# Loading the first rows on one queue, w1 in column chunks behind them, and the last stores in halves

## The chip, the cores and the metric

The kernel runs on one core of a Trainium2 chip. The metric is the device time of one execution in microseconds (us), lower is better; a number for a kernel is the median of several runs. One execution is also taken by the hardware profiler; its records, grouped in views, are what this document reads.

## The reference

The work is two branches on the same layer-normalised rows, added to the input. With 2048 rows of 640 values and a hidden width of 1536:

```python
xn = _layernorm(x, axis=-1)
a = einsum("bsd,ed->bse", xn, dft_hid_re)          # 640 x 640
b = einsum("bsd,ed->bse", xn, dft_hid_im)
y = einsum("ts,bse->bte", dft_seq_re, a) - einsum("ts,bse->bte", dft_seq_im, b)   # 2048 x 2048
h = gelu(einsum("bsd,df->bsf", xn, w1) + b1)       # 640 x 1536
return x + y + einsum("bsf,fd->bsd", h, w2) + b2   # 1536 x 640
```

Everything is float32.

## The kernel before

TensorE (PE) multiplies in a fast 32-bit format, so each operand is split into a high and a low half: ScalarE (ACT) copies the high half, VectorE (DVE) subtracts it from the value, and a product takes three matmuls, high by high, high by low and low by high (`split`, L160 and L161; `product`, L278 to L280; `hidden`, L304). The order of the work is written out by hand; no scheduler moves it.

**The front.** The first 512 rows are four tiles of 128 rows by 640 (`load_x`, 320 KB each). Before: tiles 0 and 2 are loaded by the queue of SyncE (SP), tiles 1 and 3 by that of ScalarE, each queue issuing its transfers in order. Behind them SyncE issues w1. A column of w1 is 640 inputs by 128 hidden units, held as 128 partitions by 5 chunks of 128, the partitions in four quadrants of 32; `load_w1` loads it with four transfers, one for each quadrant, and for columns 0 and 1 with eight, chunks 0 and 1 ahead of 2 to 4. The raw columns use three buffers in turn. A transfer has one of eight completion semaphores in turn, so SyncE issues one only when the transfer eight places earlier on that semaphore has landed.

While the rows come, PE runs ten warm-up matmuls on zeros (`NWARM`, L676). Then, for each tile: its mean (`ln_stats` on VectorE for tiles 0 and 2, `sum_on_act` on ScalarE for 1 and 3), the rows less the mean (`center`, L705, or L716 on ScalarE), five transposes on PE (`transpose_x`, L693) into five PSUM banks. The first column of w1 is split in two parts, chunks 0 and 1 and then 2 to 4 (L728, L729), on ScalarE and VectorE, both ahead of the splits of the five transposed banks (L160, L161). After that PE runs the units: `hidden(0)`, `hidden(1)`, `hidden(2)` of 15 matmuls each, on columns 0, 1, 2 of w1. `hidden(0)` follows the order `FIRST`, which asks for the halves as they become ready. Column 1 is split by `prep_w1(1)`, column 2 by the lines L752 and L758; behind L752 ScalarE copies the first unit's sum (L753) and spreads the row scales over a tile (L755), which PE transposes (L764, `spread`) inside `hidden(2)`, after `ASIDE` = 1 of its matmuls. From there on come the GELU of unit 0 and the first second-layer matmuls, then one unit after another with a hidden and a second-layer part. SyncE's order behind w1's columns 0 to 2 is w2's first tile, the bias b1, two more tiles of w2, then columns 3 and 4.

**The tail.** The Fourier branch works on blocks of 512 output rows; the last pair of blocks comes out as column pairs in the sums `u1`, `u2` and a fifth column. For the last block `in_two` transposes a pair in 32x32 squares on VectorE (L1332), adds it (L452) and stores it with four transfers, one for each quadrant (`store`, L1309). Before: the first pair is stored by SyncE, the second by ScalarE's queue, the fifth column by GpSimd (POOL). Last of all come two single columns of the block before (L1329, L1750), the second of which waits for PE's last matmul; each is stored by SyncE and ScalarE, two transfers each. `end` adds a saved column to a PSUM bank ahead of PE's last fifteen matmuls.

Of the kernel before, what the change touches and what calls it, by code (L numbers as in the profile page):

```python
# [10 lines left out]
F32 = mybir.dt.float32  # L11
# [5 lines left out]
Q = 4  # L17
B = 32
EPS = 1e-5
NWARM = 10  # L20
TAIL = 4
ASIDE = 1
PADL = 8


# [1 line left out]
def kernel(  # L27
# [126 lines left out]
    def split(hi, lo, src, perm=False):  # L154

        h, l, s = (hi, lo, src)
        if perm:
            h, l = chunked(hi), chunked(lo)
            s = src.rearrange("p (q c i) -> p q c i", q=Q, i=B)
        nc.scalar.activation(h, s, AF.Copy)  # L160
        nc.vector.tensor_tensor(l, s, h.bitcast(F32), op=ALU.subtract)  # L161
# [8 lines left out]
    def rows_of(ap, t):  # L170
        return ap[t * TB : (t + 1) * TB].rearrange("(n r) d -> r n d", r=B)
# [4 lines left out]
    def load_x(c, eng=nc.sync):  # L176
        xt[c] = row_tile(f"x{c}")
        eng.dma_start(xt[c], x[c * P : (c + 1) * P])  # L178
# [66 lines left out]

    W1, W2, w1r, w2r = {}, {}, {}, {}

    def load_w1(i, eng=nc.sync, cuts=(0, ND)):
        if i >= NF:
            return  # L250
        t = early.tile([P, ND, P], F32, tag="w1r", bufs=3, name=f"w1r{i}")
        w1r[i] = t
        v = w1.rearrange("(q c i) f -> q i c f", q=Q, i=B)
        for c0, c1 in zip(cuts, cuts[1:]):
            for q in range(Q):
                eng.dma_start(t[q * B : (q + 1) * B, c0:c1], v[q, :, c0:c1, i * P : (i + 1) * P])  # L256

    def load_w2(i, eng=nc.sync):
        if i >= NF:
            return  # L260
        t = early.tile([P, D], F32, tag="w2r", bufs=3, name=f"w2r{i}")
        w2r[i] = t
        eng.dma_start(t, w2[i * P : (i + 1) * P, :])
# [43 lines left out]
        return acc  # L307


    FIRST = [(0, 0), (0, 2), (1, 0), (1, 2), (0, 1), (2, 0), (2, 2), (1, 1), (3, 0), (3, 2)]  # L310
    FIRST += [(2, 1), (4, 0), (4, 2), (3, 1), (4, 1)]

    def gelu(g, acc, fill=lambda k: None):
# [338 lines left out]

    zeros = rows.tile([P, TB], F32, tag="yt", bufs=2, name="zeros")

    RB = rows.tile([P, TB], F32, tag="yt", bufs=2, name="rb")

    for c in range(NC):
        load_x(c, nc.scalar if c % 2 else nc.sync)
    for tag, size, keys in PLACES:
        t = whole[tag] = place(tag, (P, size // 4))  # L660
        for k, key in enumerate(keys):
# [1 line left out]
    nc.gpsimd.memset(eps, EPS)  # L663
    make_identity(nc, ident)
    nc.vector.memset(zeros, 0.0)
    warm = whole["as"][:, :TB]
    nc.vector.tensor_copy(warm, zeros)

    nc.scalar.activation(eps[:, 1:2], eps[:, 0:1], AF.Sqrt)
    load_w1(0, cuts=(0, 2, ND))  # L670
    load_w1(1, cuts=(0, 2, ND))

    wacc = bank(0)

    def warm_up():
        nc.tensor.matmul(wacc, warm[:, :P], warm, start=True, stop=True)  # L676

    for k in range(NWARM):
        warm_up()
    load_w1(2)  # L680
    load_w2(0)
    nc.sync.dma_start(b1c, b1.rearrange("(i p) -> p i", p=P))
    load_w2(1)
    load_w2(2)
    for j in range(ND):
        new_xt(0, j)
    tacc = [bank(3 + j) for j in range(ND)]
# [35 lines left out]
    sum_on_act(3)  # L723
    center(3, ALU.add, MV[:, 3, 5:6], 0, 2)
    center(3, ALU.add, MV[:, 3, 5:6], 2, ND)
    for lo, hi in ((0, 2 * P), (2 * P, D)):
        h, l = (W1[0][:, k, lo:hi] for k in range(2))
        nc.scalar.activation(h, first_w1[:, lo:hi], AF.Copy)  # L728
        nc.vector.tensor_tensor(l, first_w1[:, lo:hi], h.bitcast(F32), op=ALU.subtract)  # L729
    transpose_x(0, 0, ND)  # L730
    transpose_x(1, 0, ND)
    warm_up()
    for j0, j1 in ((0, 2), (2, ND)):
        transpose_x(2, j0, j1)
        transpose_x(3, j0, j1)
    for j in range(ND):
        split(XT[j][:, 0], XT[j][:, 1], tacc[j])
    load_w1(3)
    load_w1(4)
    for q in range(Q):  # L740
# [562 lines left out]
            for k in names:  # L1303
                nc.sync.dma_start(part_of(t, k), sums[t, k])

    def store(t, src, c0, c1, on_act=0, queues=None):

        for q in range(Q):
            (queues[q] if queues else nc.scalar if q >= Q - on_act else nc.sync).dma_start(  # L1309
                rows_of(out, t)[:, :, q * DQ + c0 : q * DQ + c1], src[q * B : (q + 1) * B]  # L1310
            )

    def reload(lo, w, which="xab"):
# [225 lines left out]
    def hidden_beside(b, n):  # L1539


        ta, tb = blocks[b - 1][1], blocks[b][1]
        last = b == len(blocks) - 1
        x_, y_, z_ = (banks[:, k : k + 2] for k in (X, Y, Z))
        us, vs = bank(US), bank(VS)
        ya = yo[ta]

        def s(which, k):
            return sums[(ta, tb)[which], k]

        def t2(k):
            return lambda: add(s(1, KU[k]), s(1, KV[k]), s(1, KU[k]), ALU.subtract)

        def t3(k):
            return lambda: add(s(0, KU[k]), s(1, KU[k]), s(0, KU[k]), ALU.subtract)

        def t4(k):
            return lambda: add(s(0, KV[k]), s(0, KV[k]), s(1, KU[k]), ALU.subtract)

        def columns(k):  # L1560

            return s(1 if last else 0, ("u1", "u2")[k]).rearrange("p a b -> p (a b)").rearrange("p (n e) -> p n e", n=NB)

        def load_yb(k):
            return lambda: nc.sync.dma_start(columns(k), ys[k][tb])

        def copy(dst, src):
            return lambda: nc.scalar.activation(dst, src, AF.Copy)

        def to(dst, acc, name, then=lambda: None):  # L1570


            def f():
                add_turned(dst, turned(acc, name))
                then()

            return f

        def out_a(c0, c1):
            return lambda: store(ta, ya[:, :, c0:c1], c0, c1) if last else None  # L1580

        def odd():
            yt = turned(us, f"yo_{tb}")
            add_turned(ya[:, :, 4 * B :], yt)
            add_turned(yo[tb, 4], yt)
            out_a(4 * B, DQ)()

        def in_two(k):

            acc, name = s(1, ("v2", "v1")[k]), f"yb{k}_{tb}"  # L1590

            def f():
                if name not in A:
                    A[name] = turned(acc, name)
                else:
                    add_turned(columns(k), A.pop(name))
                    out_b(k)()

            return f

        def out_b(k):
            return lambda: store(tb, columns(k), 2 * k * B, 2 * (k + 1) * B, Q if last and k == 1 else 0)

        def last_columns():

            A["end"] = A["rt2"][:, 0, 0, 0]
            nc.vector.transpose(A["end"].rearrange("p (n i) -> p n i", i=B), ya[:, :, 3 * B : 4 * B])

        yb1, yb2 = in_two(0), in_two(1)
        yb4 = to(  # L1610
            yo[tb, 4], vs, f"yb4_{tb}", lambda: store(tb, yo[tb, 4], 4 * B, DQ, queues=[nc.gpsimd] * Q if last else None)
        )
        f5s = [lambda u=u: f5(u) for u in range(2)] if not last else [lambda: None] * 2
        f6s = [lambda u=u: f6(u) for u in range(2)] if not last else [lambda: None] * 2
        v1 = lambda: add(s(1, "v1"), s(1, "v1"), x_)
        end = lambda: add(bank(X + 1), bank(X + 1), A["end"])
        pre = [v1] if n == 17 and not last else []
        post = {

            0: [lambda: gather(1, tb, "v1", z_), lambda: gather(1, tb, "v", vs, op=ALU.subtract), f5s[0]],  # L1620
            1: [f5s[1]],
            3: [to(ya[:, :, : 2 * B], x_, f"ya1_{ta}")],
            2: [last_columns] if last else [],
            4: [t2(0)],
            5: [t2(1)],
            6: [to(ya[:, :, : 2 * B], y_, f"ya2_{ta}", out_a(0, 2 * B)), t2(2)],
            7: [odd],
            8: [t3(0)],
            9: [copy(s(1, "v1"), z_), t3(1)],
            10: [t3(2)],  # L1630
            11: [t4(0)],
            12: [copy(s(1, "v2"), x_), t4(1)],
            13: [load_yb(0), t4(2), load_yb(1)] if last else [t4(2)],
            14: [lambda: add(s(1, "v2"), s(1, "v2"), z_), yb1],
            15: [yb1] if last else [load_yb(0)],
            16: [] if last else [load_yb(1)],
            17: [v1, end, yb2, yb2] if last else [yb1, yb2],
            18: [yb4] if last else [yb2],
            19: [f6s[0]],
            20: [] if last else [f6s[1], yb4],  # L1640
        }.get(n, [])
        if not last:
            if n in (12, 13):
                post.insert(0, lambda: load_g(b, (NW - 1) * ND + 13 - n))
            if n == 18:
                post[:0] = [lambda k=k: load_part(blocks[b + 1][1], k) for k in ("u1", "u")]
            if n == 20:
                post.append(lambda: load_a(put_off[0]))

                def end():  # L1650
                    to(ya[:, :, 2 * B : 4 * B], x_, f"ya3_{ta}")()
                    store(ta, ya, 0, DQ)

                later.append(end)
        return pre, post
# [129 lines left out]
```

## Time and profile before

| | before |
|---|---|
| median of 3 runs | 852.13 us (851.18 to 852.75) |
| profiled execution, own time | 852.08 us |
| its span in the profile | 850.3 us |
| granted TensorE clock | 0.999 |

The profile's page gives busy time of each engine, the chain of work that ended last and the costliest groups; other views answer for a stretch of time, a tile or an engine's waits. PEld is PE's weight load, which overlaps its matmuls; SPq and ACTq are the issue of transfers on SyncE's and ScalarE's queues. DMA share is the mean busy share of the 16 DMA engines that all queues use.

### The profile page before, as it was taken

Reading aid. Unit: us, or ns where it says so; the run is one execution under the profiler, and the core shown is the slowest. Engines: PE = TensorE matmul, PEld = TensorE weight load, DVE = VectorE, ACT = ScalarE, POOL = GpSimd, SP = SyncE. Lnnn points to the kernel's source line nnn. Section 1 sums busy time; section 2 is a strip of 40 time slices with the busy share of each in tenths; the row PEclk is TensorE's granted clock in tenths of the full one; section 3 lists DMA queues with packets and bytes.
Section 4 is the critical chain, followed back from the end, with each engine's and each line's share of the span. In section 5 each row is a group of like instructions: output and inputs, shape, how many; then the busy total and the mean of one; then the engine's idle time right before and its main releaser. Section 6 shows DMA issues by size and latency. Waiting matters only on the chain.

```text
span 850.3 us, 10328 instructions
## 1 busy us (share of the span) xinstructions
PE 841.5 (99%) x3707; PEld 694.6 (82%) x3707; DVE 666.5 (78%) x837; ACT 355.5 (42%) x499; POOL 48.4 (6%) x70
## 2 busy tenths in 40 slices
PE   8999999999999999999999999999999999999997
PEld 6888888878888888888888888888888888888885
DVE  6675766776758888779988887889967998885686
ACT  7554634456665544343444343232323433322241
POOL 0000311031211400000000000000000000000001
PEclk9999999999999999999999999999999999999999
DMA  6667699837679999858644679563855789704464
GB/s 180 187 184 193 156 224 253 197 87 186 205 247 348 353 193 173 174 129 188 154 137 110 162 234 289 145 150 98 208 163 171 253 193 229 300 19 180 126 181 96
DMA packets 207363, 158.45 MB, mean 186 GB/s; under 512 B 80976, under 2 KB 180816, under 8 KB 206800
## 3 DMA queue, kind: packets, MB, share of 16 engines
q1 hardware_dynamic: 198720, 135.38, 62.3%
q0 software_dynamic: 4080, 20.97, 6.2%
q10 hardware_dynamic: 4512, 1.44, 0.7%
q8 instruction: 29, 0.48, 0.3%
q14 instruction: 22, 0.18, 0.1%
HBM read 114.76 MB, written 42.99 MB: 186 GB/s over the span
## 4 chain that ended last, share of the span: by engine, by line
PE 98%; DMA 1%; ACT 0%; DVE 0%; SPq 0%; issue 0%; ACTq 0%
PE banks L278 29%; PE banks L279 29%; PE banks L280 29%; PE banks L304 10%; DMA x<-in_A_x_dram 1%; DMA w1r<-in_B_w_dram 0%; PE banks L336 0%; PE banks L339 0%; PE banks L337 0%; DVE yo L1750 0%; ACT xab L728 0%; ACT xtt L160 0%; PE banks L764 0%; SPq L178 0%; SPq L256 0%
## 5 line engine op out<-in xcount | busy, mean ns | idle before, releaser
L278 PE MATMUL banks<-as,xab 128*128 128x512 f32 x411 | 159.9, 389 | 0.0
L279 PE MATMUL banks<-as,xab 128*128 128x512 f32 x411 | 159.9, 389 | 0.0
L280 PE MATMUL banks<-as,xab 128*128 128x512 f32 x411 | 159.9, 389 | 0.0
L160 ACT ACTIVATE as<-r 128x1024 fp32r<-128x1024 f32 x80 | 85.0, 1062 | 177.4 <-PE banks L280 152.7
L161 DVE TENSOR_TENSOR as<-r,as 128x1024 fp32r<-128x1024 f32 x80 | 97.2, 1215 | 41.6 <-ACT as L160 41.5
L279 PEld LDWEIGHTS banks<-as,xab 128*128 128x128 f32 x411 | 77.2, 188 | 16.0
L278 PEld LDWEIGHTS banks<-as,xab 128*128 128x128 f32 x411 | 77.2, 188 | 16.0
L280 PEld LDWEIGHTS banks<-as,xab 128*128 128x128 f32 x411 | 77.2, 188 | 16.0
L278 PE MATMUL banks<-as,xc 128*128 128x512 f32 x224 | 87.1, 389 | 0.0
L279 PE MATMUL banks<-as,xc 128*128 128x512 f32 x224 | 87.1, 389 | 0.0
L280 PE MATMUL banks<-as,xc 128*128 128x512 f32 x224 | 87.1, 389 | 0.0
L160 ACT ACTIVATE as<-rt 128x1024 fp32r<-128x1024 f32 x32 | 34.0, 1063 | 70.5 <-PE banks L280 62.5
L304 PE MATMUL banks<-xtt,xab 128*128 128x512 f32 x240 | 57.2, 391 | 0.3 <-ACT xtt L160 0.3
L304 PEld LDWEIGHTS banks<-xtt,xab 128*128 128x128 f32 x240 | 44.7, 188 | 10.2 <-ACT xtt L160 0.7
L279 PEld LDWEIGHTS banks<-as,xc 128*128 128x128 f32 x224 | 42.1, 188 | 8.8
L280 PEld LDWEIGHTS banks<-as,xc 128*128 128x128 f32 x224 | 42.1, 188 | 8.7
L278 PEld LDWEIGHTS banks<-as,xc 128*128 128x128 f32 x224 | 42.1, 188 | 8.7
L161 DVE TENSOR_TENSOR as<-rt,as 128x1024 fp32r<-128x1024 f32 x32 | 38.8, 1211 | 5.3 <-ACT as L160 5.3
L160 ACT ACTIVATE as<-u 128x1024 fp32r<-128x1024 f32 (+1 forms) x24 | 22.1, 919 | 48.2 <-PE banks L280 48.2
L512 DVE STREAM_TRANSPOSE r<-raw 128x1024 f32<-128x1024 f32 x32 | 39.5, 1239 | 2.5 <-PE banks L280 1.9
L161 DVE TENSOR_TENSOR as<-u,as 128x1024 fp32r<-128x1024 f32 (+1 forms) x24 | 24.9, 1041 | 18.8 <-ACT as L160 18.8
L512 DVE STREAM_TRANSPOSE rt<-raw 128x1024 f32<-128x1024 f32 x32 | 38.8, 1230 | 0.9 <-PE banks L280 0.8
(351 smaller groups left out, 1615.9 us busy)
## 6 DMA issues: line engine op xcount, KB each, us to landing
raw<-in_A_dft_seq_re_dram SPq DMA_DIRECT2D x64, 256.0 KB, 5.6
raw<-in_A_dft_seq_im_dram SPq DMA_DIRECT2D x64, 256.0 KB, 5.1
ws<-wit SPq DMA_DIRECT2D x15, 384.0 KB, 4.6
xs<-x SPq DMA_DIRECT2D x64, 80.0 KB, 1.8
xo<-in_A_x_dram SPq DMA_DIRECT2D x16, 320.0 KB, 6.4
xab<-wit SPq DMA_DIRECT2D x13, 384.0 KB, 4.7
wit<-wstp POOLq DMA_DIRECT2D x12, 384.0 KB, 3.7
x<-in_A_x_dram SPq DMA_DIRECT2D x14, 320.0 KB, 4.5
```

Source lines behind the costliest of these rows:

```text
L160: nc.scalar.activation(h, s, AF.Copy)
L161: nc.vector.tensor_tensor(l, s, h.bitcast(F32), op=ALU.subtract)
L278: nc.tensor.matmul(acc, wh, mh, start=first, stop=False, skip_group_check=goes_on)
L279: nc.tensor.matmul(acc, wh, ml, start=False, stop=False, skip_group_check=goes_on)
L280: nc.tensor.matmul(acc, wl, mh, start=False, stop=last, skip_group_check=goes_on)
L304: nc.tensor.matmul(acc, W1[i][:, a, j * P : (j + 1) * P], XT[j][:, b], start=n == 0, stop=n == len(steps) - 1)
L512: nc.vector.transpose(held(pieces[g][2], u).rearrange("p c (n i) -> p c n i", i=B), r.rearrange("p n (c i) -> p c n i", i=B))
```

## The change

All four row tiles are issued by SyncE. For columns 0 to 7 `load_w1` issues five transfers, one for each chunk over all 128 partitions; the others keep four by quadrant, so that the number of transfers in all is the same. The zeros of the warm-up matmuls are held three times, in the three raw buffers of w1: the first six matmuls read the first, two more the second, and one after the transposes of tiles 0 and 1 the third. A column's first transfer so waits for the matmuls that read its buffer. The loads of column 2, of w2 and of the bias follow that last warm-up in the program. The second part of the first column's split moves behind the splits of two transposed banks. `FIRST` asks for the low half of bank 1 earlier, and the spread comes after two matmuls instead of one.

At the end the first pair is stored by GpSimd. The second pair is transposed, added and stored in two halves of eight row groups: the first half by SyncE and ScalarE, the second by GpSimd, with `end` between them. The fifth column's four transfers go to SyncE, ScalarE and GpSimd (two).

```diff
-NWARM = 10
+NWARM = 8
+NGATE = (6, 8)
-ASIDE = 1
+ASIDE = 2
...
-    def load_w1(i, eng=nc.sync, cuts=(0, ND)):
+    def load_w1(i, eng=nc.sync):
...
         v = w1.rearrange("(q c i) f -> q i c f", q=Q, i=B)
-        for c0, c1 in zip(cuts, cuts[1:]):
-            for q in range(Q):
-                eng.dma_start(t[q * B : (q + 1) * B, c0:c1], v[q, :, c0:c1, i * P : (i + 1) * P])
+        if i < 8:
+            for c in range(ND):
+                eng.dma_start(t[:, c], v[:, :, c, i * P : (i + 1) * P])
+            return
+        for q in range(Q):
+            eng.dma_start(t[q * B : (q + 1) * B], v[q, :, :, i * P : (i + 1) * P])
...
-    FIRST = [(0, 0), (0, 2), (1, 0), (1, 2), (0, 1), (2, 0), (2, 2), (1, 1), (3, 0), (3, 2)]
+    FIRST = [(0, 0), (0, 2), (1, 0), (1, 2), (0, 1), (1, 1), (2, 0), (2, 2), (3, 0), (3, 2)]
...
+    warms = [early.tile([P, TB], F32R, tag="w1r", bufs=3, name=f"warm{k}") for k in range(3)]
...
     for c in range(NC):
-        load_x(c, nc.scalar if c % 2 else nc.sync)
+        load_x(c)
...
-    warm = whole["as"][:, :TB]
-    nc.vector.tensor_copy(warm, zeros)
+    for warm in warms:
+        nc.vector.tensor_copy(warm, zeros)
...
-    load_w1(0, cuts=(0, 2, ND))
-    load_w1(1, cuts=(0, 2, ND))
+    load_w1(0)
+    load_w1(1)
...
-    def warm_up():
+    def warm_up(k):
+        warm = warms[sum(k >= n for n in NGATE)]
         nc.tensor.matmul(wacc, warm[:, :P], warm, start=True, stop=True)
     for k in range(NWARM):
-        warm_up()
-    load_w1(2)
-    load_w2(0)
-    nc.sync.dma_start(b1c, b1.rearrange("(i p) -> p i", p=P))
-    load_w2(1)
-    load_w2(2)
+        warm_up(k)
...
-    for lo, hi in ((0, 2 * P), (2 * P, D)):
-        h, l = (W1[0][:, k, lo:hi] for k in range(2))
-        ...
+    split_first(0, 2)
     transpose_x(0, 0, ND)
     transpose_x(1, 0, ND)
-    warm_up()
+    warm_up(NWARM)
+    load_w1(2)
+    load_w2(0)
+    nc.sync.dma_start(b1c, b1.rearrange("(i p) -> p i", p=P))
+    load_w2(1)
+    load_w2(2)
...
     for j in range(ND):
         split(XT[j][:, 0], XT[j][:, 1], tacc[j])
+        if j == 1:
+            split_first(2, ND)
...
         def out_b(k):
-            return lambda: store(tb, columns(k), 2 * k * B, 2 * (k + 1) * B, Q if last and k == 1 else 0)
+            return lambda: store(tb, columns(k), 2 * k * B, 2 * (k + 1) * B, [nc.gpsimd] * Q if last else None)
+
+        def last_two():
+            acc, yt = s(1, "v1"), A["yt"](f"yb2_{tb}")
+            d = columns(1).rearrange("p n (e i) -> p e n i", i=B)
+            v1()
+            for n in range(2):
+                m = slice(n * TB // 2, (n + 1) * TB // 2)
+                for e in range(2):
+                    nc.vector.transpose(yt[:, e, m], acc[:, e, m])
+                dn = d[:, :, n * NB // 2 : (n + 1) * NB // 2]
+                add(dn, dn, yt[:, :, m].rearrange("p e (n i) -> p e n i", i=B))
+                queues = [nc.gpsimd] * Q if n else [nc.sync, nc.scalar] * 2
+                store(tb, columns(1), 2 * B, 4 * B, queues, n * NB // 2, (n + 1) * NB // 2)
+                if n == 0:
+                    end()
...
-            yo[tb, 4], vs, f"yb4_{tb}", lambda: store(tb, yo[tb, 4], 4 * B, DQ, queues=[nc.gpsimd] * Q if last else None)
+            yo[tb, 4], vs, f"yb4_{tb}", lambda: store(tb, yo[tb, 4], 4 * B, DQ, queues=[nc.sync, nc.scalar, nc.gpsimd, nc.gpsimd] if last else None)
...
-            17: [v1, end, yb2, yb2] if last else [yb1, yb2],
+            17: [last_two] if last else [yb1, yb2],
```

More of the change, by code (lines that the diff above doesn't have):

```diff
@@ L725, with split_first @@
     center(3, ALU.add, MV[:, 3, 5:6], 2, ND)
-    for lo, hi in ((0, 2 * P), (2 * P, D)):
-        h, l = (W1[0][:, k, lo:hi] for k in range(2))
-        nc.scalar.activation(h, first_w1[:, lo:hi], AF.Copy)
-        nc.vector.tensor_tensor(l, first_w1[:, lo:hi], h.bitcast(F32), op=ALU.subtract)
+    def split_first(lo, hi):
+        h, l = (W1[0][:, k, lo * P : hi * P] for k in range(2))
+        nc.scalar.activation(h, first_w1[:, lo * P : hi * P], AF.Copy)
+        nc.vector.tensor_tensor(l, first_w1[:, lo * P : hi * P], h.bitcast(F32), op=ALU.subtract)
+    split_first(0, 2)
     transpose_x(0, 0, ND)
     transpose_x(1, 0, ND)
-    warm_up()
+    warm_up(NWARM)
[4 more added lines that the diff above has]
+    load_w2(2)
     for j0, j1 in ((0, 2), (2, ND)):
@@ L1304, in put, with store @@
                 nc.sync.dma_start(part_of(t, k), sums[t, k])
-    def store(t, src, c0, c1, on_act=0, queues=None):
+    def store(t, src, c0, c1, queues=None, n0=0, n1=NB):
         for q in range(Q):
-            (queues[q] if queues else nc.scalar if q >= Q - on_act else nc.sync).dma_start(
-                rows_of(out, t)[:, :, q * DQ + c0 : q * DQ + c1], src[q * B : (q + 1) * B]
+            (queues[q] if queues else nc.sync).dma_start(
+                rows_of(out, t)[:, n0:n1, q * DQ + c0 : q * DQ + c1], src[q * B : (q + 1) * B, n0:n1]
             )
```

## The prediction

> **What bounds the kernel now.** I read the page first: span, busy shares, the chain that ended last.
>
> ```profile
> span 850.3 us, 10328 instructions
> PE 841.5 (99%) x3707; PEld 694.6 (82%) x3707; DVE 666.5 (78%) x837; ACT 355.5 (42%) x499; POOL 48.4 (6%) x70
> PE 98%; DMA 1%; ACT 0%; DVE 0%; SPq 0%; issue 0%; ACTq 0%
> ```
>
> TensorE (PE) carries the span. The waits view of PE for the whole run has only three rows (who waited, for whom, us in total, times, longest); the windows view behind it (stretch, us, then busy time of PE, PEld, DVE, ACT, POOL, granted clock, DMA share, GB/s) shows the two ends:
>
> ```profile
> PE banks L676 <- DVE as L667: 1.9, 1, 1.9
> PE banks L693 <- DVE xp L705: 0.5, 1, 0.5
> PE banks L304 <- ACT xtt L160: 0.3, 1, 0.3
> ```
>
> ```profile
> 0.00:10.00 10.00, 7.41 (x31) 5.43 (x31) 5.39 (x14) 5.18 (x10) 0.94 (x8) 1.00 0.53 174
> ...
> 844.00:850.30 6.30, 0.28 (x2) 0.00 (x0) 0.72 (x1) 0.00 (x0) 0.62 (x1) 0.92 0.68 114
> ```
>
> All three waits lie ahead of the first real matmul; from there PE never waits until its last one at about 844.3. So the time is three pieces: the front up to the dense run, the dense run, the tail of 6.0 us. The change leaves the dense matmuls as they are, so only front and tail can move it, and whatever delays PE in the first units goes straight into the total. The chain of waits for the first 12 us (start, us, what) says what ends last in the front:
>
> ```profile
> 1.19 5.58 DMA x<-in_A_x_dram
> ...
> 7.14 1.93 DMA w1r<-in_B_w_dram
> ...
> 9.18 0.53 ACT xab L728
> 9.70 0.49 ACT xtt L160
> ...
> 10.24 1.90 PE banks L304 x7
> ```
>
> The third row tile lands at 6.77. A w1 transfer on SyncE waited for that, was issued at 7.14 and landed 1.93 us later; the second part of w1's first split (L728) waited for it, and the first split of the transposed rows (L160) stands behind that on ScalarE. The timeline gives the work around it:
>
> ```profile
> 1.91 4.54 PE L676 MATMUL banks<-as 128*128 128x512 f32 x10 [1.91 <-DVE as L667]
> ...
> 7.96 1.14 DVE L705 TENSOR_SCALAR xp<-x,mv 128x640 f32<-128x640 f32 x3
> ...
> 9.61 2.53 ACT L160 ACTIVATE xtt<-banks 128x512 fp32r<-128x512 f32 x5
> ...
> 9.73 0.56 DVE L729 TENSOR_TENSOR xab<-w1r,xab 128x384 fp32r<-128x384 f32 x1 [0.30 <-ACT xab L728]
> ...
> 10.22 3.08 DVE L161 TENSOR_TENSOR xtt<-banks,xtt 128x512 fp32r<-128x512 f32 x5
> ...
> 13.06 0.74 ACT L160 ACTIVATE xab<-w1r 128x640 fp32r<-128x640 f32 x1 [0.92 <-DMA w1r<-in_B_w_dram]
> ...
> 13.85 3.50 PEld L304 LDWEIGHTS banks<-xtt,xab 128*128 128x128 f32 x16 [0.31 <-ACT xab L160]
> ...
> 15.62 0.72 ACT L752 ACTIVATE xab<-w1r 128x640 fp32r<-128x640 f32 x1
> ...
> 17.61 0.60 PE L764 MATMUL banks<-ident,ab 128*128 128x128 f32 x4
> ```
>
> Two deadlines come out: column 1 of w1 is split at 13.06 and opens the second hidden unit at 13.85; column 2 is split at 15.62 (L752), the two ScalarE copies behind it end in the spread (L764) at 17.61, 1.99 us later. PE waits at neither for long, so both are nearly exact.
>
> **Part 1: rows alone, w1 behind them.** The first w1 chunk now takes the buffer that six warm-up matmuls read, so it is issued when the sixth ends: ten took 4.54 us, so six end at about 1.91 + 6 x 0.45 + 0.2 = 4.8, issue 4.9. Behind that wait stand all of SyncE's later issues; the rows are ahead of it. By 6.77 the four row tiles (1.31 MB) and six w1 pieces (0.23 MB) have moved. At full flow
>
> ```profile
> 4.00:5.00 1.00, 1.00 (x3) 0.77 (x3) 0.00 (x0) 0.09 (x1) 0.00 (x0) 1.00 1.04 410
> ```
>
> 410 GB/s, taking 0.23 MB away is worth 0.56 us: last rows at about 6.2, and since one queue delivers them in turn, 0.8 us (0.33 MB) apart, the third at 5.4 instead of 6.77. Today the last centering ends at 7.96 + 1.14 = 9.10, 2.33 us behind the third tile; so it would end at 7.7, and the first split of the transposed rows could start at 7.9 instead of 9.61. VectorE then needs 0.61 us to its first low half, 3.08 us for five of them, and 0.56 us for w1's second low half, which now stands between them: 12.15. With one matmul (0.23 us) behind it the second hidden unit opens at 12.4 instead of 13.85: 1.4 us gained, if w1 is there. The bounds are 0.8 (rows 0.6 later on the single queue) and 2.0 (the low half hidden). Two warm-ups fewer, the spread one matmul later and the order of FIRST cost nothing: PE waits for rows in the first case, and its matmuls are the same.
>
> **Part 2: is w1 there?** Issue is cheap: two of the old pieces take 0.90 us of SyncE, 0.47 apart.
>
> ```profile
> 8.56 0.90 SPq L256 DMA_DIRECT2D w1r<-in_B_w_dram  x2
> ```
>
> Fifteen chunks for columns 0 to 2 are issued from 4.9 to 11.6. But their form is new. Every old piece names 32 rows on both sides; the new one has a source list of 4 blocks of 32 rows of 512 bytes against 128 partitions. If a transfer is dealt over the 16 DMA engines along its outermost list, the old pieces fill all 16 and a chunk fills four, with 32 pieces of 512 bytes each. No transfer of the run before begins with a list shorter than 32, so no row decides it; I price both. What one engine needs for 512 bytes is in these rows (the first holds w1 pieces alone, the second mostly the 512-byte runs of the raw loads, saturated):
>
> ```profile
> 11.00:11.50 0.50, 0.50 (x3) 0.40 (x3) 0.50 (x2) 0.50 (x2) 0.00 (x0) 1.00 0.35 99
> ...
> 330.00:345.00 15.00, 15.00 (x68) 12.39 (x67) 13.94 (x16) 8.03 (x11) 0.00 (x0) 1.00 1.24 218
> ```
>
> First row: 0.35 x 16 = 5.6 engine-us for 99 KB, 193 pieces, 29 ns each. Second: 218 GB/s is 426 pieces a us, 27 per engine, 38 ns each. A floor is 410 GB/s over 16, 20 ns. On four engines a chunk so takes 0.93 us (0.64 to 1.2), twice its issue distance: the engines become the pace. A lone piece lands 1.93 us after issue, 0.17 of it data (6 x 29 ns), so the first chunk lands at 4.9 + 1.76 + 0.93 = 7.6, the tenth at 16.0, the fifteenth at 20.6. The second hidden unit then opens at 16.0 + 0.74 + 0.05 = 16.8, not 13.85; column 2 is split at 20.6 instead of 15.62, and the spread follows 1.99 us later: 22.6 against 17.61, **5.0 us lost**. The 1.4 of part 1 is eaten, because w1 is now last. At 0.64 the loss is 0.7 us, at 1.2 it is 9.1. What queues behind on those four engines (w2's first tile, 8 rows of 2560 bytes per engine, 0.8 us) is wanted only behind the spread. Column 3 comes after three such tiles, the bias (1 us by estimate) and five more chunks: 20.6 + 2.4 + 1 + 4.65 = 28.7, split at 29.4. It opens the unit that starts at 24.67 now,
>
> ```profile
> 24.67 3.56 PE L304 MATMUL banks<-xtt,xab 128*128 128x512 f32 x15
> ```
>
> so at 29.7: just in time, and later columns have 6.8 us of PE work each against 4.65. So the loss is paid once. I take 29 ns, the row with the same pieces, and four engines, because the short list is the one thing in which these transfers differ from all others.
>
> The Trainium skill bears on this: "DMA: Bandwidth & Descriptors", section "Why a DMA increments its semaphore by 16 and not by 1", says that the number of engines is the largest up to 16 that divides the outermost size of both sides, which would be 4 here. By it the sum is the 5.0 us lost; by the old pieces' behaviour it would be 1.4 gained; no run here shows it yet.
>
> **Part 3: the tail.** The rows:
>
> ```profile
> 837.64 1.23 DVE L1332 STREAM_TRANSPOSE yb<-v 128x1024 f32<-128x1024 f32 x1
> ...
> 838.91 1.23 DVE L452 TENSOR_TENSOR u<-u,yb 128x1024 f32<-128x1024 f32 x1
> ...
> 840.17 2.10 ACTq L1309 DMA_DIRECT2D out_dram<-u  x4
> ...
> 841.79 0.72 DVE L1329 STREAM_TRANSPOSE yt<-banks 128x512 f32<-128x512 f32 x1
> ...
> 841.99 2.64 POOL L1309 DMA_DIRECT2D out_dram<-y  x4 [545.19 <-DVE y L452]
> ...
> 842.54 0.69 DVE L452 TENSOR_TENSOR yo<-yo,yt 128x512 f32<-128x512 f32 x1
> ...
> 843.26 3.14 SPq L1309 DMA_DIRECT2D out_dram<-yo  x4
> ...
> 844.32 0.72 DVE L1750 STREAM_TRANSPOSE yo<-banks 128x512 f32<-128x512 f32 x1 [1.09 <-PE banks L280]
> ```
>
> ```profile
> out_dram<-u SPq DMA_DIRECT2D x4, 128.0 KB, 2.3
> ...
> out_dram<-yo SPq DMA_DIRECT2D x4, 64.0 KB, 3.2
> ```
>
> The last two are DMA issues of the last 22 us with the median from issue to landing. One transpose of 1024 becomes four of 256 (0.46 each, from 0.72 and 1.23 for 512 and 1024), one addition of 1024 two of 512: 1.84 + 1.38 against 2.46, 0.7 us more VectorE work ahead of the second-to-last column's add. Its stores go out at 843.96, still before the last transpose at 844.32, which PE sets; the 1.09 us that VectorE idles there is the cover. The first half of the pair leaves 1.5 us earlier, its second half and half of the fifth column go through GpSimd later, at 0.66 an issue (2.64 for four), the last at 844.6, landing by 848. The first pair's store moves to GpSimd too, at 834, where it delays nothing: GpSimd idled until 841.99. The last stores are issued at 845.05 as now. They land 3.2 us after issue, 2.3 where the engines are free: at best 0.9 gained. At worst the 0.95 us of engine work that the halves bring past 844 (a quarter MB of 256-byte runs, and the column's part) lies ahead of them: 0.9 lost. The window behind 844 holds 0.68 x 6.3 = 4.3 us of engine work, so the engines are nearly full until the end; I take 0.3 lost.
>
> The same page, "Issuing engines are not separate DMA queues", says that queues share the 16 engines and more of them save issue time alone; the full engines agree, and by it the third queue gains nothing here.
>
> **Sum.** 852.08 (the profiled execution's own time, 1.8 over its span and 0.05 under the median of three) + 5.0 + 0.3 = **857.4**.
>
> **Rivals.** (1) Sixteen engines carry a chunk. The tenth then lands by 9.2 + 1.9 = 11.1, the second unit opens at 12.4: 852.08 - 1.4 + 0.3 = 851.0; with the tail's better end 849.8. For it: nothing in the run shows an engine left out. Against: the list of four. It decides where a chunk's data take under 0.6 us. (2) Four engines at the saturated 38 ns: 9.1 + 0.3, 861.5. Against: twelve engines stand idle in those microseconds. (3) Four engines at 20 ns: +0.7 + 0.3, 853.1. Against: no row shows 512 bytes that fast. (4) The change does not gate: if the chunks left at 1.7 as now, the rows would again share the flow, and in the four-engine case w1 would land 3 us sooner: 854.4.
>
> **How the numbers follow.** A measurement here tells 0.2%, 1.7 us, from no change. Chances: forecast and (4) together 0.68, own range 854 to 860; (2) 0.08; (3) 0.05, within 1.7; (1) 0.19, of which 0.10 with the tail or the rows at the better end lies over 1.7 below, 0.09 within. So faster 0.10, same 0.14, slower 0.76. The range 851.0 to 861.5 takes in the bounds of the forecast, (3) and half of (1).
>
> **What would show it.** Right: the windows of 6 to 20 us show a DMA share of about 0.25 (four of 16) with some 70 GB/s, the split of column 2 (L752, L764 in the new file) starts near 20.6 behind a wait for w1, and PE has two waits, near 15 and 21. Wrong: w1 chunks landing 2 us after issue throughout, ScalarE never waiting for w1, the second unit open before 13. The row part is right if the first statistics start by 3.9 and the last centering ends by 8. The tail is right if the last matmul is followed by 5.1 to 6.9 us.

## The result, and the profile after

The changed kernel takes 859.56 us (median of six runs, 857.46 to 861.39) against 852.01 us for the kernel before in the same comparison (851.18 to 852.75): 1.0088 times, 95% interval 1.007 to 1.0106. The profiled execution took 860.2 us, its span is 858.3, 8.0 us more than before. Every position in this text is from a profiled execution; "+x" is against the same point of the kernel before.

The page's head and chain, and the waits view of PE for the whole run (who waited, for whom, us in total, times, longest):

```profile
span 858.3 us, 10341 instructions
PE 844.4 (98%) x3705; PEld 693.4 (81%) x3705; DVE 667.3 (78%) x843; ACT 355.6 (41%) x499; POOL 52.6 (6%) x76
PE 78%; DMA 7%; DVE 5%; SPq 4%; issue 3%; ACT 2%; POOL 0%; ACTq 0%; DVEq 0%; POOLq 0%
```

```profile
PE banks L308 <- ACT xtt L161: 2.0, 2, 1.2
PE banks L683 <- DVE warm L673: 1.9, 1, 1.9
PE banks L308 <- ACT xab L161: 1.3, 1, 1.3
PE banks L282 <- ACT banks L869: 1.0, 1, 1.0
PE banks L284 <- DVE rt L162: 0.9, 1, 0.9
PE banks L776 <- ACT ab L767: 0.3, 1, 0.3
PE banks L308 <- ACT xab L764: 0.2, 1, 0.2
```

The chain was 98% PE; now 16% of it runs through loads, VectorE and SyncE's queue. PE waits eight times instead of three, 7.6 us in all instead of 2.7, and two of these waits (1.0 and 0.9) are not at the front. The windows view at the front (stretch, us, busy of PE, PEld, DVE, ACT, POOL, clock, DMA share, GB/s), then the timeline:

```profile
8.00:10.00 2.00, 1.24 (x10) 0.93 (x8) 0.86 (x3) 1.31 (x3) 0.00 (x0) 1.00 0.20 59
...
14.00:16.00 2.00, 1.09 (x5) 0.52 (x3) 0.54 (x1) 0.44 (x1) 0.00 (x0) 1.00 0.29 87
...
24.00:26.00 2.00, 2.00 (x9) 1.45 (x9) 0.69 (x1) 1.16 (x3) 0.00 (x0) 1.00 0.29 87
```

```profile
6.89 1.17 DVE L707 TENSOR_SCALAR xp<-x,mv 128x640 f32<-128x640 f32 x3
...
4.87 10.70 SPq L257 DMA_DIRECT2D w1r<-in_B_w_dram  x15
...
15.56 0.74 ACT L161 ACTIVATE xab<-w1r 128x640 fp32r<-128x640 f32 x1 [1.97 <-DMA w1r<-in_B_w_dram]
...
19.47 0.74 ACT L764 ACTIVATE xab<-w1r 128x640 fp32r<-128x640 f32 x1 [1.25 <-DMA w1r<-in_B_w_dram]
...
16.35 3.69 PE L308 MATMUL banks<-xtt,xab 128*128 128x512 f32 x15 [1.26 <-ACT xab L161]
...
21.26 0.66 PE L776 MATMUL banks<-ident,ab 128*128 128x128 f32 x4 [0.27 <-ACT ab L767]
...
28.30 3.56 PE L308 MATMUL banks<-xtt,xab 128*128 128x512 f32 x15
```

The rows do come earlier: the last centering ends at 8.06 instead of 9.10. Then w1 is late: a flat 87 GB/s, 64 KB in 0.75 us, and SyncE issues a chunk every 0.71 us (10.70 / 15). Column 1 opens the second hidden unit at 16.35 (+2.50), the spread comes at 21.26 (+3.65), column 3 opens its unit at 28.30 (+3.63).

The other 4.5 us are lost further on. SyncE's queue in the timeline of both kernels, before first, up to the rows of the second block (stores of `xs`, then loads of x):

```profile
28.95 3.68 SPq L203 DMA_DIRECT2D xs<-x  x8
33.36 1.40 SPq L178 DMA_DIRECT2D x<-in_A_x_dram  x2
```

```profile
29.73 7.14 SPq L257 DMA_DIRECT2D w1r<-in_B_w_dram  x10
36.97 0.56 SPq L267 DMA_DIRECT2D w2r<-in_B_w_dram  x1
37.62 4.59 SPq L204 DMA_DIRECT2D xs<-x  x8
42.80 1.14 SPq L179 DMA_DIRECT2D x<-in_A_x_dram  x2
```

The queue is 8.67 us behind there (37.62 against 28.95). VectorE and PE before, then VectorE, ScalarE and PE after, in the same view:

```profile
37.49 0.88 DVE L185 BATCH_NORM_STATS2 st<-x 128x6 f32<-128x320 f32 x2
...
51.87 3.56 PE L304 MATMUL banks<-xtt,xab 128*128 128x512 f32 x15
...
843.89 0.39 PE L280 MATMUL banks<-as,xab 128*128 128x512 f32 x1
```

```profile
45.75 0.89 DVE L186 BATCH_NORM_STATS2 st<-x 128x6 f32<-128x320 f32 x2 [3.61 <-DMA x<-in_A_x_dram]
...
46.80 0.64 DVE L324 TENSOR_TENSOR ab<-banks,rb 128x512 f32<-128x512 f32 x1
...
47.47 0.72 ACT L326 ACTIVATE ab<-ab,b1c 128x512 f32<-128x512 f32 x1 [6.30 <-DVE ab L324]
...
87.11 0.71 DVE L239 STREAM_TRANSPOSE zt<-z 128x512 f32<-128x512 f32 x1 [3.40 <-DMA z<-xs]
...
35.30 4.10 PE L308 MATMUL banks<-xtt,xab 128*128 128x512 f32 x15
...
49.53 4.11 PE L308 MATMUL banks<-xtt,xab 128*128 128x512 f32 x15
...
56.88 3.56 PE L308 MATMUL banks<-xtt,xab 128*128 128x512 f32 x15
...
103.14 0.50 PE L284 MATMUL banks<-hs,rt 128*128 128x512 f32 x1 [0.87 <-DVE rt L162]
...
188.64 0.50 PE L282 MATMUL banks<-xtt,tw 128*128 128x512 f32 x1 [1.05 <-ACT banks L869]
...
852.03 0.39 PE L284 MATMUL banks<-as,xab 128*128 128x512 f32 x1
```

VectorE stands 3.61 us at the statistics of the second block's rows, where it did not wait before; the multiply ahead of the gelu (L324) is behind them on the same engine, and ScalarE idles 6.30 us for it (at most 3.9 between 20 and 60 us in the kernel before). PE falls further behind in steps. The fifteen matmuls of column 4's unit take 4.10 us instead of 3.56, which is ahead of VectorE's stand, and those of column 6's 4.11, which is behind it; column 7's unit opens at 56.88 (before at 51.87: +5.01). The remaining 3.1 us come between 91 and 189 us, for the most part at the two waits shown at 103.14 and 188.64. Ahead of them VectorE had stood another 3.40 us (87.11) for a load of `z` from `xs`, which SyncE issued from 78.65 on instead of 70.77. So the queue's lateness and PE's run side by side, but the trace does not show for each step that the one makes the other. By the last matmul, 852.03 against 843.89, PE is at +8.14. Behind that one, 5.9 us are left, as before (6.0).

### The profile page after: what moved, and what is told of

The parts are those of the page before. It is cut to its first block, busy times and chain, and to the rows that moved or that the text cites. A ratio compares the mean times of both kernels' runs of the same rounds, so it can differ in the third digit from the quotient of the medians.

```text
span 858.3 us, 10341 instructions
## 1 busy us (share of the span) xinstructions
PE 844.4 (98%) x3705; PEld 693.4 (81%) x3705; DVE 667.3 (78%) x843; ACT 355.6 (41%) x499; POOL 52.6 (6%) x76
## 4 chain that ended last, share of the span: by engine, by line
PE 78%; DMA 7%; DVE 5%; SPq 4%; issue 3%; ACT 2%; POOL 0%; ACTq 0%; DVEq 0%; POOLq 0%
PE banks L282 26%; PE banks L283 26%; PE banks L284 26%; DMA wit<-wst 2%; DMA x<-in_A_x_dram 1%; DMA w2r<-in_B_w_dram 1%; SPq L257 1%; DMA rq<-in_B_w_dram 1%; DMA w1r<-in_B_w_dram 1%; SPq L392 1%; DMA xs<-x 1%; SPq L204 1%; DVE xtt L162 1%; DVE st L186 0%; PE banks L683 0%
## 5 line engine op out<-in xcount | busy, mean ns | idle before, releaser
L308 PE MATMUL banks<-xtt,xab 128*128 128x512 f32 x240 | 59.0, 395 | 3.8 <-ACT xtt L161 2.0
```

The lines of the kernel that those rows point to most:

```text
L308: nc.tensor.matmul(acc, W1[i][:, a, j * P : (j + 1) * P], XT[j][:, b], start=n == 0, stop=n == len(steps) - 1)
```

## The experiments

Theory A: a chunk occupies four DMA engines and 0.71 us of SyncE's queue, and the time goes in two places, the first columns' lateness and the queue's lateness behind them. Theory B: the chunks cost only the front's 3.6 us, once, and the rest comes from the rows, the gate or the tail. The kernels below stand beside runs of the kernel before that took 851.24 to 851.37 us in the median.

| run | median us | ratio to before (95%) | hidden(3) opens | last matmul | first store of `xs` issued |
|---|---|---|---|---|---|
| before (profile) | | | 24.67 | 843.89 | 28.95 |
| changed | 859.56 | 1.0088 (1.007 to 1.0106) | +3.63 | +8.14 | 37.62 |
| e1 quarters | 853.98 | 1.0033 (1.002 to 1.0046) | +0.87 | +0.80 | 29.21 |
| e2 rows in order | 851.62 | 1.0004 (0.9995 to 1.0014) | -0.52 | +1.32 | 27.85 |
| e3 chunks in columns 0, 1 | 854.25 | 1.0034 (1.0021 to 1.0047) | +2.28 | +2.27 | 29.12 |
| e5 before, with chunks | 857.74 | 1.0075 (1.006 to 1.009) | +2.66 | +5.05 | 34.98 |
| e4 chunks in columns 2 to 7 | 859.80 | 1.0097 (1.0082 to 1.0112) | +3.10 | +7.09 | 36.20 |
| e6 before, queue delayed | 857.47 | 1.0075 (1.006 to 1.009) | -0.76 | +5.00 | 37.07 |
| e7 rows on GpSimd | 858.27 | 1.008 (1.0063 to 1.0097) | +3.62 | +5.87 | 32.11 (GpSimd) |
| f3 rows ahead | 862.19 | 1.0124 (1.0108 to 1.014) | +3.16 | +10.94 | 31.92 |
| e9 quarters, fewer | 851.15 | 0.9998 (0.9989 to 1.0007) | -0.55 | -0.56 | 27.01 |

**Quarters again, everything else kept (e1).**

```diff
-        if i < 8:
-            for c in range(ND):
-                eng.dma_start(t[:, c], v[:, :, c, i * P : (i + 1) * P])
-            return
-        for q in range(Q):
-            ...
+        cuts = (0, 2, ND) if i < 2 else (0, ND)
+        for c0, c1 in zip(cuts, cuts[1:]):
+            for q in range(Q):
+                eng.dma_start(t[q * B : (q + 1) * B, c0:c1], v[q, :, c0:c1, i * P : (i + 1) * P])
```

> The changed kernel with w1 loaded by quarters of the partitions again (columns 0 and 1 in two parts, eight transfers each, the other columns in four), its rows on SyncE alone, gated warm-up, split first column and new tail kept. Theory A (the five-column chunks alone cost the time: each holds four DMA engines and SyncE's queue 0.71 us, and the queue's delay of 8.7 us by the second block's rows becomes the kernel's): 850.5 to 852.5 us, hidden(2) opening by 14, the second block's rows fetched near 29 us. Theory B (the chunks cost only the 3.6 us seen by hidden(3), paid once; the other 4.4 us come from the rows on one queue, the gate or the tail): 855 to 857 us.

Measured 853.98 us, between the ranges of the two theories: of the ratio's 0.0088 the chunks are 0.0055. The rest of the change does not come out at 851 with these quarters; PE's timeline shows why:

```profile
14.69 4.17 PE L306 MATMUL banks<-xtt,xab 128*128 128x512 f32 x17 [0.92 <-ACT xab L161]
```

Column 1, split in two, needs eight issues behind column 0's eight, and all of them start 3.2 us later than before (4.86 against 1.68): it is late by 0.9. The profiled run is the fastest of this kernel (852.98); the others go up to 855.3, which the profile doesn't explain.

**The same chunks, read from consecutive rows (e2).** Same number of issues, bytes and pieces; only the source's list differs. The rows of w1 so arrive in another order and this kernel leaves out putting them right: it does the same work on a permuted w1.

```diff
-                eng.dma_start(t[:, c], v[:, :, c, i * P : (i + 1) * P])
+                eng.dma_start(t[:, c], w1[c * P : (c + 1) * P, i * P : (i + 1) * P])
```

> The changed kernel with the same 40 chunks of 64 KB in 512 B pieces issued at the same places, but each taken from 128 consecutive rows of w1 (so the values of w1 are permuted; the arithmetic after it is unchanged in kind). Only the source's list changes, from four blocks of 32 rows to one of 128. If the four blocks keep the transfer on four of 16 engines (theory A), the issues come every 0.4 to 0.5 us, a chunk lands in under 2.5 us, the rate in 8 to 16 us goes from 87 to over 140 GB/s, and the time is 850.5 to 853 us. If the price is in five issues to a column of 64 KB each, however their list reads (rival), the pitch stays at 0.71 us, 87 GB/s, and the time at 858 to 861 us.

SyncE's issues in the timeline of e2, and its windows view at 10 us, where only chunks are under way:

```profile
4.87 6.98 SPq L257 DMA_DIRECT2D w1r<-in_B_w_dram  x15
```

```profile
10.00:12.00 2.00, 2.00 (x10) 1.37 (x9) 2.00 (x5) 2.00 (x5) 0.00 (x0) 1.00 0.53 140
```

The issues come every 0.47 us instead of 0.71 (6.98 / 15), the rate in 8 to 12 us is 134 to 140 GB/s where it was 59 to 84 and never went over 87 with chunks alone, 140 being what one 64 KB chunk in 0.47 us gives, a chunk lands 2.2 us after its issue in the median, and the time is 851.62, that of the kernel before. So neither 64 KB pieces nor five issues to a column cost anything here: the list of four blocks does, and it slows the issuing queue along with the data. (The profiled run is this kernel's slowest, 853.51, with two late waits of 0.9 and 0.6 us; the others lie from 851.26 to 852.16.)

**Chunks in columns 0 and 1 alone (e3), in columns 2 to 7 alone (e4), and in the kernel before (e5).** The edits set the bound in `load_w1` to `i < 2`, to `2 <= i < 8` with e1's quarters for the first two columns, and put the chunk form into the kernel before.

> The changed kernel with chunks for columns 0 and 1 alone, columns 2 to 7 by quarters. The prediction's step 'the loss is paid once' (columns 3 to 7 cost nothing in chunks): 857.5 to 859.5 us, as only column 2's own lateness of about 1 us goes. Theory A (every chunk costs SyncE's queue some 0.25 us more than a quarter of a column's bytes, whatever the column): ten chunks of 40 stay, hidden(2) opens near 16, the second block's rows are fetched 3 to 4 us later than before instead of 8.7, and the time is 853.5 to 856 us.

> The counterpart of the run with chunks in columns 0 and 1: the changed kernel with quarters for columns 0 and 1 and chunks for columns 2 to 7. Theory A, sharpened (two losses: the first columns' lateness at the front, and SyncE's queue, 0.71 us to a chunk, bringing the second block's rows so late that VectorE, which takes its instructions in order, waits for them ahead of the gelus): the front loses about 1 us as with quarters, SyncE reaches the second block's rows at 35 to 37 us instead of 29, VectorE waits 2 to 4 us for x near 42, and the time is 856 to 859 us. If the loss is only the front's and paid once: 853 to 855 us.

> The kernel before with the chunk form for columns 0 to 7 and nothing else of the change: rows on two queues, no gate, old tail. Theory A: the whole loss, 859 to 862 us, since rows and gate gave about 1 us back. Theory B (chunks cost 3.6 us, the rest lies in the other parts): 855 to 857 us.

The table separates two losses. With chunks in columns 0 and 1 the kernel is 2.28 us late at hidden(3) and 2.27 at the end: the front's loss alone is paid once. SyncE reaches the second block's rows in time there (29.12, not 3 to 4 us late as expected: these ten chunks take 6.25 us of its queue, the sixteen transfers that e4 has for the same two columns 7.39), and between 20 and 130 us VectorE waits for x once, for 0.4 us (0.8 in the kernel before). With chunks in columns 2 to 7 alone the time is that of the whole change, above the range expected: the front loses 3.10, since column 2 is late all the same, and 4.0 more go behind it (VectorE in the timeline of e4):

```profile
44.54 0.89 DVE L186 BATCH_NORM_STATS2 st<-x 128x6 f32<-128x320 f32 x2 [2.86 <-DMA x<-in_A_x_dram]
```

e5 lies between the two theories' ranges: 6.5 us with no gate, rows or tail. The changed kernel is 0.0013 of the ratio above e5, which their intervals do not separate, and its queue is 2.6 us later at the second block's rows (37.62 against 34.98), as its first w1 issue is (4.87 against 1.65). e5 also loses time to a halved clock, which the changed kernel does not (last section), so the two do not show what the other parts are worth beside the chunks.

**A delay of the queue and nothing else (e6).**

```diff
+    idle = [dram.tile([1, D], F32, name=f"idle{k}") for k in range(16)]
...
+        if i == 0:
+            for k in range(16):
+                nc.sync.dma_start(idle[k], x[k : k + 1])
```

> The kernel before with sixteen one-row copies within DRAM (2.5 KB each, for nothing) on SyncE's queue ahead of the second block's rows, which delays that queue by about 6.5 us and changes nothing ahead of 29 us; no chunk anywhere. Theory A: hidden(3) opens at 24.7 as before, VectorE waits for x near 41 us, and the kernel ends 4 to 6 us later (queue delay less 0.5 to 1 us of slack): 855 to 857.5 us. Rival (the later loss comes from w1's columns on four engines, not from the queue's delay): 851 to 852.5 us.

```profile
26.88 10.10 SPq L938 DMA_DIRECT2D idle<-in_A_x_dram  x16
37.07 4.08 SPq L204 DMA_DIRECT2D xs<-x  x8
...
44.21 0.89 DVE L186 BATCH_NORM_STATS2 st<-x 128x6 f32<-128x320 f32 x2 [8.07 <-DMA x<-in_A_x_dram]
...
47.98 5.71 PE L305 MATMUL banks<-xtt,xab 128*128 128x512 f32 x15 [3.52 <-ACT xab L161]
```

No chunk, nothing late at the front (-0.76), and yet 857.47 us (the timeline of e6 above: SyncE, VectorE, PE). VectorE waits for x as in the changed kernel, only longer, and behind it the split of column 6 comes late: PE stands 3.52 us, and its next fifteen matmuls take 5.71 us, for the most part because of a halved clock (last section). That a late queue at this place is enough to cost several us is shown. That the changed kernel loses its 4.5 us by the same steps is not: there the loss is spread over column 4's unit, column 6's and the stretch from 91 to 189 us, and the clock stays up.

**Taking the rows out from behind the chunks (e7, f3).** In e7 the first block's stores of `xs` and the loads of x chunks 4 to 7 go through GpSimd; in f3 they stay on SyncE ahead of columns 6 and 7.

```diff
-            load_w1(i + 6)
+            if i < 2:
+                first_block(i)
+            load_w1(i + 6)
             load_w2(i + 4)
-            if i != 8:
+            if i not in (0, 1, 8):
                 first_block(i)
```

> The changed kernel, all chunks kept, with the second block's rows (the first block's stores of xs and the loads of x chunks 4 to 7) issued by GpSimd's queue instead of SyncE's. Theory A: the rows no longer stand behind the chunks, VectorE's wait of 3.6 us near 42 is gone, hidden(3) still opens near 28.3, and the time falls to 854.5 to 856.5 us; what of the second block still stands behind SyncE's queue (w2, the third group of rows) may keep up to 1 us. Rival (late columns themselves): 858 to 861 us.

> The changed kernel, all chunks kept, with the second block's rows (stores of xs, loads of x chunks 4 to 7) put ahead of columns 6 and 7 of w1 on SyncE's queue instead of behind them. Theory A (the rows' lateness behind the chunks makes the later loss): SyncE reaches the rows near 33 us instead of 37.6, VectorE's wait of 3.6 us at 42 is gone or under 1 us, hidden(3) stays at 28.3, columns 6 and 7 are still in time, and the time falls by 2.5 to 4.5 us, to 855 to 857 us. Rival (late columns of w1 themselves, or the chunks' traffic): 858.5 to 861 us.

Both missed. GpSimd (timeline of e7) has the stores out from 32.11, but its loads wait for them to land, and x comes no sooner (45.51 against 45.75):

```profile
40.08 0.58 POOL L179 DMA_DIRECT2D x<-in_A_x_dram  x1 [3.83 <-DMA xs<-x]
...
45.51 0.89 DVE L186 BATCH_NORM_STATS2 st<-x 128x6 f32<-128x320 f32 x2 [3.65 <-DMA x<-in_A_x_dram]
```

So e7 did not take away what it was to take away, and tells nothing for or against. f3 did: the wait of 3.6 us is gone. But now column 7 of w1 comes last, issued from 49.20 on (ScalarE and VectorE in the timeline of f3):

```profile
56.43 0.74 ACT L161 ACTIVATE xab<-w1r 128x640 fp32r<-128x640 f32 x1 [4.93 <-DMA w1r<-in_B_w_dram]
57.20 0.82 DVE L162 TENSOR_TENSOR xab<-w1r,xab 128x640 fp32r<-128x640 f32 x1 [4.97 <-ACT xab L161]
```

VectorE stands 4.97 us, for something else, and the kernel is slower than the change as it was. This corrects theory A: it is not the rows that are special. Everything up to 60 us comes through one queue, in order, to engines that take it in order; with 40 chunks that keep it 0.57 to 0.68 us each (in f3), where e2's keep it 0.47 to 0.54, something on it is late. That the order only chooses what is the reading that fits e6, e7 and f3; no run delays each load by itself.

**Without the chunks: what gate, rows and tail are worth (e9, f1, f2, f4).** e9 is e1 with only column 0 in two parts, so that column 1 takes four issues (`i < 1` in the cuts). f1 is e9 without the gate (the warm-up on a tile of its own, as before), f2 e9 with the old tail, f4 e9 with column 0 whole too.

> The changed kernel with w1 by quarters, column 0 alone in two parts (eight transfers), column 1 in four instead of eight, so that SyncE reaches column 2 about 1.9 us sooner; rows on SyncE, gate, split and new tail kept. If the quarters run's 2.7 us came from the second column's wait (0.92 us at 14.7) and from the queue behind it: 850.5 to 852 us. If they come from the rows, the gate or the tail: 853 to 854.5 us.

> The version with quarters (column 0 in two parts, others in four transfers) without the gate: the warm-up works on a tile of its own, so w1's transfers are issued right behind the rows' at 2.6 us instead of 4.9. If the gate gives nothing: 850.5 to 851.5 us, the last centering later than 8.1 us but SyncE's queue 2 us ahead. If keeping w1 out of the rows' way is worth its us: 851.8 to 852.6 us.

> The version with quarters (column 0 in two parts, others in four transfers; rows on SyncE, gate) with the old tail: the last block's second pair stored whole by ScalarE and its last column by GpSimd. The prediction's step (new tail costs 0.3 us, between -0.9 and +0.9): 850.5 to 851.2 us, 0 to 0.3 us below the same version with the new tail, with 5.7 to 6.1 us behind the last matmul either way. Rival (the halves and the third queue help): 851.5 to 852 us.

> The version with quarters with column 0 whole too (four transfers to every column): SyncE's queue is 1.9 us further ahead, but the first column's first two parts land with the rest of it. If the queue's pace still sets the time: 849.5 to 850.8 us. If the first matmul waits for the whole column: hidden(0) opens 0.3 to 0.8 us later than 9.2 and the time is 851.2 to 852 us.

Measured: e9 851.15; f1 851.74, 1.0001 (0.9992 to 1.001); f2 851.60, 1.0002 (0.9993 to 1.0011); f4 851.81, 1.0004 (0.9995 to 1.0013). All four equal the kernel before, and their intervals overlap one another; f2 and f4 lie in the range of the second guess made for each and f1 between its two, but their medians are 0.4 to 0.7 us above e9's, which is not told apart from nothing here. Four issues fewer than e1 are worth 2.8 us in the medians (1.4 at the last matmul of the profiled executions, +0.80 to -0.56): column 1's wait is gone and the queue is at the rows at 27.01. Gate and tail cannot be told from nothing. In e9 the front is 0.55 us ahead and stays so to the last matmul, yet of it 0.1 us arrives in the medians. No version beats the kernel before beyond what can be measured.

## Why the prediction was right, and where its steps were not

The forecast of 857.4 us in 851.0 to 861.5, slower, held (859.56). Its mechanism, one transfer's short list on four engines, is shown by e2 as the cause of the loss. That the number came so close is in part luck, since a term that was too large stood in for one that was left out (Sum, below). The steps one by one:

- **Four engines (part 2): right.** The share of 0.29 and 87 GB/s stand for the 0.25 and 70 that were named. By an estimate from these rows 0.29 of 16 engines is 4.6, or 3.7 if a full engine counts 1.24 as in the saturated stretch of 330 to 345 us; four lies between. The Trainium skill's "DMA: Bandwidth & Descriptors", section "Why a DMA increments its semaphore by 16 and not by 1", says that a transfer runs on the largest number of engines, up to 16, that divides the slowest dimension of both sides. Both traces agree: list of 4, 87 GB/s; list of 128, 140 GB/s at a share of 0.53, there at the pace of the issues.
- **0.93 us to a chunk, 5.0 us at the spread: mis-sized.** It measured 0.75 us (23.4 ns to 512 bytes on each of four engines, between the 20 and the 29 that were weighed). The chunks did not run at that pace from the start (59 GB/s in 8 to 10 us, 87 later): the second unit opened at 16.35 (16.8 predicted), column 2 was split at 19.47 (20.6), the spread came at 21.26 (22.6): +3.65 instead of +5.0.
- **"Issue is cheap", 0.47 us apart: failed.** This was measured on the old form. A chunk on four engines keeps SyncE's queue 0.71 us; on sixteen, 0.47 (e2).
- **"So the loss is paid once": failed, and it is the larger error.** The working compared each column's 4.65 us of chunks with PE's 6.8 us per unit, and left out that the same queue must bring w2, `xs` and the second block's x between the columns. For column 3 the step was right: it was split at 26.45 (29.4 named), and its unit at +3.63 is no later than the spread at +3.65. From there on the queue fell 8.67 us behind, VectorE stood 3.61 us, and 4.5 us were lost after hidden(3) (8.14 - 3.63). e3 shows the case in which the step holds, e4 that it fails for columns 2 to 7, and e6 that a late queue alone can do it; how the 4.5 us divide among the late loads stays open.
- **Part 1: right in itself, and eaten.** First statistics at 3.73 (3.9 was named); the last centering ends at 8.06, just past the 8 that was named, and 1.0 us sooner than before instead of 1.4. In e9, with w1 by quarters, the front gains 0.55 us at hidden(3), less than the bounds of 0.8 to 2.0, because column 1 of w1 is still last (its split starts at 12.34). Without the gate (f1) it gains 1.0 us, w1's first issue coming at 2.60 instead of 4.86: in these executions the rows on one queue bring the gain, and the gate gives part of it back. Neither shows in the medians.
- **Part 3: within its bounds.** 5.9 us behind the last matmul (5.1 to 6.9 named); VectorE's idle time ahead of the last transpose shrinks from 1.09 to 0.67 us, so the cover held. The +0.3 is not to be seen: f2 against e9 has no measurable difference.

```profile
852.45 0.72 DVE L1778 STREAM_TRANSPOSE yo<-banks 128x512 f32<-128x512 f32 x1 [0.67 <-PE banks L284]
```

- **Sum.** 5.0 + 0 + 0.3 against 3.6 + 4.5 - 0.1 in the profiled execution: one term too large, one left out; the first covered 1.4 of the 4.5. With the first at its measured size the working would have said 856.0; the measured 859.56 is 3.6 above that, inside a range that was kept wide for slower engines (38 ns, 861.5) and not for a late queue. Rival 1 gave 851.0 for sixteen engines; e2 and e9, which are that case, measured 851.62 and 851.15. Rival 4, that the change does not gate and loses less: the change did gate (first chunk issued at 4.87, 4.9 named). e5, without gate, rows and tail, measured 857.74, 3.3 above the rival's 854.4; 2.4 of it were lost behind hidden(3) (5.05 - 2.66), for that figure too left the queue out.

## What to carry to other kernels

Read the outermost list of both sides of a transfer before its size: here 64 KB with a list of four took 0.75 us of data and 0.71 us of its queue, and with a list of 128 the kernel lost nothing. When a stream of loads gets slower, add up the whole queue that it shares to the last thing that is needed from it, not only the stream against its own consumer; an engine that takes its work in order turns one late load into a wait for everything behind it. And moving the late load forward doesn't help while the queue as a whole is late; fewer issues did (e1 to e9: four fewer, 2.8 us in the medians).

## What the runs showed of the hardware that was not expected

A pause of PE cost twice in two runs. In e5 PE idles 2.23 us before its first real matmul (its timeline, first below), in e6 3.52 us; behind both, the granted clock falls to half for about 3.4 us (windows view of e5 and of e6; the clock is the third figure from the end):

```profile
11.53 4.83 PE L308 MATMUL banks<-xtt,xab 128*128 128x512 f32 x13 [2.23 <-ACT xtt L160]
```

```profile
12.00:13.00 1.00, 1.00 (x4) 0.85 (x3) 1.00 (x3) 1.00 (x3) 0.00 (x0) 0.50 0.29 87
```

```profile
50.00:52.00 2.00, 2.00 (x6) 1.61 (x5) 1.08 (x3) 0.81 (x2) 0.00 (x0) 0.50 0.59 164
```

In e6 the fifteen matmuls behind the pause take 5.71 us instead of 3.56, so a wait of 3.52 became a loss of 5.67. Of the added 2.15, half of the 3.4 us, 1.7, can be the clock; the rest is about what column 4's and column 6's units lose in the changed kernel at full clock (4.10 and 4.11). The pauses of up to 1.26 us in the changed kernel, and of 1.6 and 1.9 us in f3, left the clock at 1.00. The Trainium skill's "TensorE: Matmul & The Clock Gate", section "Part 1: The HAM clock gate (the "warmup" mystery)", has the clock halved behind an idle window of about 3.4 us; here 2.23 us were enough once. Whether there is a limit between 1.9 and 2.23 us, or something besides the pause's length decides, no run here shows.
